# Attention's products as plain 32-bit matmuls, with P times V in column halves

## The chip, the cores and the metric

One core of a Trainium2 chip runs the whole program. The metric is the device time of one execution in microseconds (us), the median of several runs; lower is better. TensorE is called PE in the rows, its weight load PEld, VectorE DVE, ScalarE ACT, GpSimd POOL and SyncE SP.

## The reference

Causal attention over 2 batches, 12 heads, 448 positions and a head size of 64, then two feed-forward layers on its 896 x 768 output:

```python
scores = scale * np.matmul(q, k.transpose(0, 1, 3, 2))
scores = np.where(mask, -1000000000.0, scores)
scores = scores - np.max(scores, axis=-1, keepdims=True)
attn = np.exp(scores)
attn = attn / (np.sum(attn, axis=-1, keepdims=True) + 1e-09)
attn_out = np.matmul(attn, v)
x = attn_out.transpose(0, 2, 1, 3).reshape(896, 768)
x = (1 / (1 + np.exp(-(x @ w_gate))) * (x @ w_val)) @ w_out   # 768 -> 1536 -> 768
h = x @ w_in                                                 # 768 -> 2048
out = (h * np.clip(h + 3, 0, 6) / 6) @ w_out2                # 2048 -> 768
```

q, k and v arrive in 32 bits, the weights in 64 bits.

## The kernel before

Every large product is made of three matmuls. An operand is split into a high part of reduced precision (type fp32r) and the rest, low, also fp32r; `TERMS` (line 22) lists high times high, high times low and low times high, and the product low times low is left out. The attention, the part that changes, works on 12 pairs of heads (`NP`), and both heads of a pair lie side by side on the 128 partitions.

For each pair these steps run, with a short key for each:

- `Lq`, `Lk`, `Lv` (`load`, line 238): SP issues two DMAs for each of q, k, v.
- `Tq`, `Tk` (`t_pe`, line 273): TensorE transposes q and k, 4 pieces each; `Th` and `Tl` (lines 284 and 291) make the high part on ACT and the low part on DVE.
- `Vh`, `Vl` (`v_hi`, `v_lo`, lines 262 and 268): POOL splits v into tiles `vpad` whose other half is zero, so that one matmul serves both heads; these zeros are set once at the start (line 586), half on POOL and half on DVE.
- `S0`, `S1` (`s_pe`, line 299): the scores of four query tiles of 64, 128, 128 and 128 rows against 64, 192, 320 and 448 keys. Each of the three terms is a pair of matmuls on 64 partitions, one for each head (line 309); two or four small bf16 matmuls (line 320) add the causal mask.
- `M`, `E`, `R`, `N` (lines 330 to 356): row maximum on DVE, exponential and row sum on ACT with a small addition at line 343, reciprocal on DVE, division on POOL.
- `C0` to `C3` (`c_pe`, line 358): 16 TensorE transposes of the probabilities, in key chunks of 64 (both heads on the partitions), two chunks in one bank; `H` (line 374) copies the high part out on ACT, `J` (line 380) the low part on DVE.
- `D0` to `D3` (`d_pe`, line 388): P times V, 7 chunks of three matmuls with 448, 384, ... 64 columns, each with all 128 partitions and all 128 output rows.
- `Xh`, `Xl` (lines 406 and 409): the result's parts on ACT and DVE.

The order of all steps is a list written out by hand: a key for each step (`PERIOD`, `SHIFT`, `AT`, `OWN`), and the steps are issued in the order of their keys as far as dependences and buffer rings allow (lines 546 to 568). Three weight tiles of the first layer are decoded in between (`W`, `Wa` to `Wg`), matmuls of that layer that need only the first batch run late in the attention (`F`, 6 steps for each of two tiles, the matmul at line 190), and matmuls on an idle tile (`Z`, line 486) fill the start. After the attention come the two feed-forward layers, line 594 to the end, which the change doesn't touch; weights are decoded there on ACT and DVE while TensorE multiplies (lines 190, 744, 1197).

Of the kernel before, what the change touches and what calls it, by code (L numbers as in the profile page):

```python
# [31 lines left out]
def kernel(  # L32
# [178 lines left out]
    with tc.manual_schedule():  # L211

        with ExitStack() as actx:
            def pool(name, bufs, **kw):
# [11 lines left out]
            identf = const.tile([P, P + D], F32, name="identf")  # L226
# [5 lines left out]
            vpad = [  # L232
                [const.tile([P, NC, P], F32R, name=f"vpad{i}_{x}") for x in range(2)]
                for i in range(NV)
            ]
            live = {}

            def load(p, nm):
                b, hp = divmod(p, NPAIR)
                if nm == "v":  # L240
                    t = p_raw.tile([P, NC, D], F32, tag=nm, name=nm)
                    for j in range(2):
                        nc.sync.dma_start(
                            out=t[j * D : (j + 1) * D],
                            in_=v[b, 2 * hp + j].rearrange("(c p) d -> p c d", p=D),
                        )
                    live[nm, p] = t
# [11 lines left out]
            def halves_of(t):  # L259
                return [t[j * D : (j + 1) * D, :, j * D : (j + 1) * D] for j in range(2)]  # L260

            def v_hi(p):
                for j, hi in enumerate(halves_of(vpad[p % NV][0])):
                    nc.gpsimd.tensor_scalar(
                        hi, live["v", p][j * D : (j + 1) * D], 1.0, 1.0, op0=ALU.mult, op1=ALU.mult
                    )

            def v_lo(p):
                raw = live.pop(("v", p))
                for j, (hi, lo) in enumerate(zip(*(halves_of(t) for t in vpad[p % NV]))):  # L270
                    nc.gpsimd.tensor_sub(lo, raw[j * D : (j + 1) * D], hi.bitcast(F32))
# [12 lines left out]
            def t_hi(p, nm):  # L284
                hi = p_qk.tile([P, S], F32R, tag=nm + "h", name=nm + "h")
                nc.scalar.activation(
                    hi, live["tr", p, nm], AF.Copy, scale=SCALE if nm == "q" else 1.0
                )
                live[nm + "h", p] = hi

            def t_lo(p, nm):
                lo = p_qk.tile([P, S], F32R, tag=nm + "l", name=nm + "l")
                nc.vector.scalar_tensor_tensor(
                    lo, live.pop(("tr", p, nm)), SCALE if nm == "q" else 1.0,
                    live[nm + "h", p].bitcast(F32), op0=ALU.mult, op1=ALU.subtract,
                )
                live[nm + "l", p] = lo

            def s_pe(p, ts):
                both = ps_a.tile([P, 2, 512], F32, tag="m", name="s")  # L300
                off = 0
                for t in ts:
                    rows, n = Q1[t] - Q0[t], Q1[t]
                    ps = both[:, :, off : off + n]
                    off += n
                    for i, (a, c) in enumerate(TERMS):
                        for j in range(2):
                            r = slice(j * D, (j + 1) * D)
                            nc.tensor.matmul(  # L309
                                ps[:, j],  # L310
                                lhsT=live["q" + "hl"[a], p][r, Q0[t] : Q0[t] + P],
                                rhs=live["k" + "hl"[c], p][r, :n],
                                start=(i == 0),
                                stop=(i == 2),
                            )

                    for h in range(rows // D):
                        for j in range(2):
# [4 lines left out]
                                start=False, stop=True, skip_group_check=True,  # L323
                            )
                    live["s", p, t] = ps[:rows]

            def column(tag, t):
                return p_sm.tile([P, 2], F32, tag=tag, name=tag)[: Q1[t] - Q0[t]]

            def s_max(p, t):  # L330
                nm = column("nm", t)
                nc.vector.tensor_reduce(nm, live["s", p, t], axis=AX.X, op=ALU.max, negate=True)  # L332
                live["nm", p, t] = nm

            def s_exp(p, t):
                ps, nm, sm = live.pop(("s", p, t)), live.pop(("nm", p, t)), column("sm", t)
                pr = p_p.tile([P, Q1[t] // D, 2, D], F32, tag=f"pr{t}", name="pr")[: Q1[t] - Q0[t]]
                for j in range(2):
                    nc.scalar.activation(  # L339
                        pr[:, :, j], ps[:, j].rearrange("p (c d) -> p c d", d=D), AF.Exp,  # L340
                        bias=nm[:, j : j + 1], accum_out=sm[:, j : j + 1],
                    )
                nc.scalar.activation(sm, sm, AF.Copy, bias=1e-9)
                live["pr", p, t], live["sm", p, t] = pr, sm

            def s_rcp(p, t):
                sm, rc = live.pop(("sm", p, t)), column("rc", t)
                nc.vector.reciprocal(rc, sm)  # L348
                live["rc", p, t] = rc

            def s_nrm(p, t):
                pr, rc = live["pr", p, t], live.pop(("rc", p, t))
                for j in range(2):
                    nc.gpsimd.tensor_scalar(  # L354
                        pr[:, :, j], pr[:, :, j], rc[:, j : j + 1], 1.0, op0=ALU.mult, op1=ALU.mult
                    )

            def c_pe(p, g):
                ps = ps_pt.tile([P, 512], F32, tag="pt", name="pt")
                for c, off in GROUPS[g]:  # L360
                    for t in range(NQ):
                        if Q1[t] > c * D:


                            r, rows = max(0, c * D - Q0[t]), Q1[t] - Q0[t]
                            o = off + Q0[t] + r - c * D
                            nc.tensor.transpose(  # L367
                                ps[:, o : o + rows],
                                live["pr", p, t][:, c].rearrange("p j d -> p (j d)"),
                                identf[:rows, r : r + rows],  # L370
                            )
                live["pt", p, g] = ps

            def c_hi(p, g):
                m = WIDTH[g]
                hi = p_pt.tile([P, 512], F32R, tag="pth", name="pth")
                nc.scalar.copy(hi[:, :m], live["pt", p, g][:, :m])
                live["pth", p, g] = hi

            def c_lo(p, g):  # L380
                m = WIDTH[g]
                lo = p_pt.tile([P, 512], F32R, tag="ptl", name="ptl")
                nc.vector.tensor_sub(
                    lo[:, :m], live.pop(("pt", p, g))[:, :m], live["pth", p, g][:, :m].bitcast(F32)
                )
                live["ptl", p, g] = lo

            def d_pe(p, g):
                if g == 0:
                    live["pav", p] = ps_1.tile([P, S], F32, tag="pav", name="pav")  # L390
                pt = live.pop(("pth", p, g)), live.pop(("ptl", p, g))
                for c, off in GROUPS[g]:
                    for m, (a, e) in enumerate(TERMS):
                        nc.tensor.matmul(  # L394
                            live["pav", p][:, c * D :],
                            lhsT=vpad[p % NV][a][:, c],
                            rhs=pt[e][:, off : off + S - c * D],
                            start=(c == 0 and m == 0),
                            stop=((c, off) == GROUPS[-1][-1] and m == 2),
                        )  # L400
# [13 lines left out]
            GROUPS, WIDTH, chunks = [], [], list(range(NC))  # L414
            while chunks:
                GROUPS.append([])
                WIDTH.append(0)
                for c in list(chunks):
                    if len(GROUPS[-1]) < 2 and WIDTH[-1] + max(S - c * D, P) <= 512:
                        GROUPS[-1].append((c, WIDTH[-1]))  # L420
                        WIDTH[-1] += S - c * D
                        chunks.remove(c)
# [5 lines left out]
            PERIOD = 33902  # L428
            SHIFT = [
                -9916, -3016, 760, 4313, 10984, 14552, 19678, 24941, 28538, 34564, 37386, 44110,  # L430
            ]
            AT = {
# [831 lines left out]
```

## Time and profile before

| | us |
|---|---|
| median of 3 runs (598.39 to 600.19) | 599.24 |
| the profiled execution | 598.94 |
| its span, first to last instruction | 597.0 |
| PE busy in it | 585.6 |

The profile is of one execution. Its span is 1.9 us shorter than that execution's time, and the profiled execution lies 0.3 us under the median. The busy time of PE comes from modelled ends of overlapping matmuls; the start-to-start time of two matmuls, read from a timeline or from a chain, says what each really takes.

### The profile page before, as it was taken

What the parts mean: (1) busy time and instruction counts of PE and PEld (TensorE: products, weight loads), DVE (VectorE), ACT (ScalarE), POOL (GpSimd) and SP (SyncE); (2) the same over time, 40 slices, a digit from 0 to 9 for tenths busy, and PEclk for the clock granted to TensorE, in tenths of its full rate; (3) what the DMA queues carried; (4) which work ended last, traced back from release to release, by engine and by line L of the source; (5) the groups of instructions that cost most, each with busy time, mean ns of one, the idle gap of its engine ahead of it and who ended that gap; (6) DMA issues with size and microseconds to landing.
All of it is one profiled execution on the core that took longest, in us unless ns stands there. A gap on an engine that the chain in (4) does not pass through costs nothing.

```text
span 597.0 us, 9165 instructions
## 1 busy us (share of the span) xinstructions
PE 585.6 (98%) x3436; PEld 536.0 (90%) x3436; DVE 477.0 (80%) x733; ACT 345.2 (58%) x680; POOL 136.6 (23%) x201
## 2 busy tenths in 40 slices
PE   9999999999999999999999999999999999999997
PEld 5887888999998999898999999988998899999997
DVE  6899988578798898899867788888999988867601
ACT  4998999445665666658343332486777555433200
POOL 2988998601111111110000000012222000000000
PEclk9999999999999999999999999999999999999999
DMA  7664314047986767673344433467978424437002
GB/s 174 158 147 109 86 32 122 2 132 184 264 187 173 208 161 182 171 181 110 99 135 159 143 122 107 111 158 172 245 192 207 133 57 133 128 105 246 7 0 93
DMA packets 86684, 82.64 MB, mean 138 GB/s; under 512 B 35312, under 2 KB 77040, under 8 KB 86640
## 3 DMA queue, kind: packets, MB, share of 16 engines
q1 hardware_dynamic: 80448, 64.50, 36.3%
q0 software_dynamic: 6192, 17.57, 16.0%
q8 instruction: 27, 0.44, 0.3%
q14 instruction: 17, 0.14, 0.1%
HBM read 61.73 MB, written 2.75 MB: 108 GB/s over the span
## 4 chain that ended last, share of the span: by engine, by line
DVE 38%; PE 38%; ACT 18%; issue 5%; DMA 1%; SPq 0%; ACTq 0%; DVEq 0%; POOLq 0%
PE w L744 14%; PE m L1197 12%; DVE b L128 7%; DVE b L134 6%; PE pav L394 4%; DVE lo L158 4%; DVE b L124 4%; ACT hi L153 3%; ACT pr L339 3%; ACT b L115 3%; PE pt L367 2%; DVE g L1165 2%; DVE raw L120 2%; PE s L309 2%; DVE g L182 2%
## 5 line engine op out<-in xcount | busy, mean ns | idle before, releaser
L1197 PE MATMUL m<-hi,g 128*128 128x384 f32 x448 | 114.0, 335 | 0.6 <-DVE g L1165 0.6
L153 ACT CAST hi<-b 128x768 fp32r<-128x768 f32 x35 | 29.0, 835 | 105.6 <-DVE b L134 101.3
L1197 PEld LDWEIGHTS m<-hi,g 128*128 128x128 f32 x448 | 80.8, 188 | 1.2 <-DVE g L1165 1.2
L1197 PE MATMUL m<-lo,g 128*128 128x384 f32 x224 | 75.0, 335 | 0.4 <-DVE lo L158 0.4
L744 PE MATMUL w<-T,hi 128*128 128x448 f32 x252 | 71.9, 367 | 1.4 <-ACT g2r L761 1.4
L190 PE MATMUL m<-g,hi 128*128 128x448 f32 x288 | 70.1, 365 | 0.0
L128 DVE SCALAR_TENSOR_TENSOR b<-b,raw 128x768 int32<-128x768 int32 x68 | 67.0, 985 | 2.2
L134 DVE SCALAR_TENSOR_TENSOR b<-raw,b 128x768 int32<-128x768 int32 x68 | 66.2, 974 | 2.3
L115 ACT ACTIVATE b<-raw 128x768 f32<-128x768 f32 x68 | 61.2, 904 | 0.0
L190 PEld LDWEIGHTS m<-g,hi 128*128 128x128 f32 x288 | 54.1, 188 | 4.3
L124 DVE TENSOR_SCALAR b<-b 128x768 f32<-128x768 f32 x68 | 38.5, 566 | 23.4 <-ACT b L115 23.0
L158 DVE TENSOR_TENSOR lo<-b,hi 128x768 fp32r<-128x768 f32 x35 | 33.4, 958 | 28.1 <-ACT hi L153 28.0
L144 POOL DMA_DIRECT2D lo<-S x26 | 25.2, 971 | 130.9 <-ACT lo L143 110.7
L744 PEld LDWEIGHTS w<-T,hi 128*128 128x128 f32 x252 | 46.9, 188 | 6.0 <-ACT g2r L761 2.1
L354 POOL TENSOR_SCALAR pr<-pr,rc 128x320 f32<-128x320 f32 (+3 forms) x96 | 45.4, 489 | 16.7 <-DVE rc L348 14.3
L190 PE MATMUL m<-x,hi 128*128 128x448 f32 x192 | 48.9, 367 | 0.0
L744 PE MATMUL w<-T,lo 128*128 128x448 f32 x126 | 46.3, 367 | 0.9 <-DMA lo<-raw 0.6
L339 ACT ACTIVATE pr<-s,nm 128x192 f32<-128x192 f32 (+3 forms) x96 | 44.4, 470 | 2.6 <-DVE nm L332 1.6
L1197 PEld LDWEIGHTS m<-lo,g 128*128 128x128 f32 x224 | 42.0, 188 | 0.7 <-DVE lo L158 0.7
L394 PE MATMUL pav<-pth,vpad 128*128 128x448 f32 (+6 forms) x168 | 41.2, 311 | 0.1
L190 PE MATMUL m<-g,lo 128*128 128x448 f32 x144 | 40.9, 366 | 0.0
L190 PEld LDWEIGHTS m<-x,hi 128*128 128x128 f32 x192 | 35.9, 188 | 2.8
(140 smaller groups left out, 1249.4 us busy)
## 6 DMA issues: line engine op xcount, KB each, us to landing
raw<-in_moe_w_out_dram SPq DMA_DIRECT2D x28, 768.0 KB, 4.4
raw<-in_moe_w_in_dram SPq DMA_DIRECT2D x16, 768.0 KB, 4.7
lo<-S POOLq DMA_DIRECT2D x26, 384.0 KB, 4.3
raw<-in_moe_w_gate_dram SPq DMA_DIRECT2D x12, 768.0 KB, 5.0
raw<-in_moe_w_val_dram SPq DMA_DIRECT2D x12, 768.0 KB, 5.1
q<-in_q_dram SPq DMA_DIRECT2D x24, 112.0 KB, 2.9
k<-in_k_dram SPq DMA_DIRECT2D x24, 112.0 KB, 3.2
v<-in_v_dram SPq DMA_DIRECT2D x24, 112.0 KB, 2.8
```

What stands on the lines that cost most here:

```text
L115: nc.scalar.activation(b, words(u)[0].bitcast(F32), AF.Copy, scale=REBIAS)
L124: nc.vector.tensor_scalar(b, b, UPPER_MAX, -UPPER_MAX, op0=ALU.min, op1=ALU.max)
L128: nc.vector.scalar_tensor_tensor(bi, bi, 3, words(u)[1], op0=ALU.logical_shift_left, op1=ALU.bitwise_or)
L134: nc.vector.scalar_tensor_tensor(bi, words(u)[0], -(2 ** 31), bi, op0=ALU.bitwise_and, op1=ALU.bitwise_or)
L153: nc.scalar.copy(hi, part_t[u])
L158: nc.vector.tensor_sub(lo, part_t.pop(u), split_t[u][0].bitcast(F32))
L190: nc.tensor.matmul(ps[:, b, :S], lhsT=w[a][:, i * P : (i + 1) * P], rhs=x(c, k0 + i, b), start=(first and i == 0 and n == 0), stop=(last a ...
L339: nc.scalar.activation(pr[:, :, j], ps[:, j].rearrange("p (c d) -> p c d", d=D), AF.Exp, bias=nm[:, j : j + 1], accum_out=sm[:, j : j + 1],)
L354: nc.gpsimd.tensor_scalar(pr[:, :, j], pr[:, :, j], rc[:, j : j + 1], 1.0, op0=ALU.mult, op1=ALU.mult)
L394: nc.tensor.matmul(live["pav", p][:, c * D :], lhsT=vpad[p % NV][a][:, c], rhs=pt[e][:, off : off + S - c * D], start=(c == 0 and m == 0), ...
L744: nc.tensor.matmul(ps, lhsT=w[a][:, k * P : (k + 1) * P], rhs=x[:, c, i], start=(first and i == 0 and n == 0), stop=(i == HK - 1 and n == ...
L1197: nc.tensor.matmul(po[t], lhsT=g2[2 * s + i][a][:, t * P : (t + 1) * P], rhs=w[e][:, i * HC : (i + 1) * HC], start=(s == 0 and i == 0 and ...
```

## The change

Scores and P times V are each one matmul on plain 32-bit operands in place of three on split ones. For the scores there are then 2 matmuls for each query tile, one a head, after the mask's matmuls instead of before them. For P times V the key chunks become one of 64 keys and three of 128 keys. The chunk of 64 still serves both heads with one matmul; a chunk of 128 takes two matmuls, one a head, that use all 128 partitions and write 64 output partitions each: the two column halves of the array. These are 7 matmuls with 448, 384, 384, 256, 256, 128 and 128 columns. The transposes of the probabilities stay 16.

The splits of v, the low parts of q, k and P, and the high copies go; q comes out by ACT, k by DVE, two of the four groups of transposed probabilities by ACT and two by DVE. V goes by four DMAs a pair straight into three rotating 32-bit tiles, whose zeros are 6 blocks of 64 x 64 instead of 12 of 64 x 448. The addition and the reciprocal of the row sums handle two query tiles at once. The idle tile's matmuls read a constant, and the list of keys is another one.

```diff
--- before.py
+++ after.py
-            vpad = [
-                [const.tile([P, NC, P], F32R, name=f"vpad{i}_{x}") for x in range(2)]
-                for i in range(NV)
-            ]
+            vs = [const.tile([P, NQ, 2, D], F32, name=f"v{i}") for i in range(NV)]
...
             def load(p, nm):
                 if nm == "v":
-                    t = p_raw.tile([P, NC, D], F32, tag=nm, name=nm)
                     for j in range(2):
-                        nc.sync.dma_start(
-                            out=t[j * D : (j + 1) * D],
-                            in_=v[b, 2 * hp + j].rearrange("(c p) d -> p c d", p=D),
-                        )
+                        chunks = v[b, 2 * hp + j].rearrange("(c p) d -> p c d", p=D)
+                        for x in range(2):
+                            nc.sync.dma_start(
+                                out=vs[p % NV][x * D : (x + 1) * D, x != j :, j],
+                                in_=chunks[:, x != j :: 2],
+                            )
...
-            def v_hi(p):
-            def v_lo(p):
-            def t_hi(p, nm):
-            def t_lo(p, nm):
+            def t_out(p, nm):
+                t = live[nm + "t", p] = p_qk.tile([P, S], F32, tag=nm + "t", name=nm + "t")
+                if nm == "q":
+                    nc.scalar.activation(t, live.pop(("tr", p, nm)), AF.Copy, scale=SCALE)
+                else:
+                    nc.vector.tensor_copy(t, live.pop(("tr", p, nm)))
...
             def s_pe(p, ts):
-                    for i, (a, c) in enumerate(TERMS):
-                        for j in range(2):
-                            r = slice(j * D, (j + 1) * D)
-                            nc.tensor.matmul(
-                                ps[:, j],
-                                lhsT=live["q" + "hl"[a], p][r, Q0[t] : Q0[t] + P],
-                                rhs=live["k" + "hl"[c], p][r, :n],
-                                start=(i == 0),
-                                stop=(i == 2),
-                            )
...
+                for t in ts:
+                    for j in range(2):
+                        r = slice(j * D, (j + 1) * D)
+                        nc.tensor.matmul(
+                            live["s", p, t][:, j],
+                            lhsT=live["qt", p][r, Q0[t] : Q0[t] + P],
+                            rhs=live["kt", p][r, : Q1[t]],
+                            start=False, stop=True, skip_group_check=True,
+                        )
...
+            def s_eps(p, g):
+                sm = live["sm", p, g]
                 nc.scalar.activation(sm, sm, AF.Copy, bias=1e-9)
...
-            def c_hi(p, g):
-            def c_lo(p, g):
-            def d_pe(p, g):
+            def c_out(p, g):
+                m, ps = WIDTH[g], live.pop(("pt", p, g))
+                t = live["pth", p, g] = p_pt.tile([P, 512], F32, tag="pth", name="pth")
+                if g % 2:
+                    nc.vector.tensor_copy(t[:, :m], ps[:, :m])
+                else:
+                    nc.scalar.copy(t[:, :m], ps[:, :m])
+
+            def d_pe(p, d):
+                if d == 0:
                     live["pav", p] = ps_1.tile([P, S], F32, tag="pav", name="pav")
+                pav, pt = live["pav", p], {g: live.pop(("pth", p, g)) for g in DSTEPS[d]}
+                for i, j, off, g in sorted((*b, g) for g in DSTEPS[d] for b in GROUPS[g]):
+                    w, r, x = S - Q0[i], slice(j * D, (j + 1) * D), vs[p % NV][:, i]
+                    nc.tensor.matmul(
+                        pav[r, Q0[i] :] if i else pav,
+                        lhsT=x[:, j] if i else x.rearrange("p j d -> p (j d)"),
+                        rhs=pt[g][:, off : off + w],
+                        start=(i == 0), stop=True, skip_group_check=True,
+                    )
...
+            GROUPS = [
+                [(0, 0, 0)], *([(1, j, 0), (3, j, S - Q0[1])] for j in range(2)),
+                [(2, j, j * (S - Q0[2])) for j in range(2)],
+            ]
+            DSTEPS = [(0,), (1, 2), (3,)]
...
-            PERIOD = 33902
+            PERIOD = 21033
```

## Rows read from the trace of the kernel before

**Rows 1.** The page: busy time, share of the span and instructions by engine.
```profile
PE 585.6 (98%) x3436; PEld 536.0 (90%) x3436; DVE 477.0 (80%) x733; ACT 345.2 (58%) x680; POOL 136.6 (23%) x201
```

**Rows 2.** Stretches: length, busy PE, PEld, DVE, ACT, POOL, granted clock, DMA share, GB/s.
```profile
0.00:58.45 58.45, 55.67 (x496) 42.99 (x496) 49.26 (x102) 47.06 (x159) 43.26 (x77) 1.00 0.62 148
58.45:119.68 61.23, 61.23 (x548) 54.55 (x549) 48.97 (x101) 49.83 (x171) 51.26 (x82) 1.00 0.24 61
...
83.67:92.13 8.46, 8.46 (x85) 7.41 (x84) 6.99 (x17) 7.78 (x28) 7.96 (x15) 1.00 0.21 48
119.68:250.00 130.32, 129.70 (x640) 119.82 (x640) 112.95 (x159) 79.58 (x110) 20.35 (x21) 1.00 0.73 186
```

**Rows 3.** The chain that ended last, 100 to 300 us: start, us, what.
```profile
106.13 1.30 PE m L190 x6
...
112.27 3.65 PE m L190 x18
...
116.79 2.87 PE pav L394 x21
...
251.09 22.24 PE w L744 x108
```

**Rows 4.** The same chain over one pair of heads, 74.67 to 83.13 us, by line.
```profile
by line: PE pav L394 35.5%; PE s L309 25.8%; PE pt L367 23.5%; PE tr L277 11.1%; PE s L320 4.1%
```

**Rows 5.** PE's timeline, 59.6 to 66 us: start, us, instruction.
```profile
59.77 0.28 PE L309 MATMUL s<-kh,ql 64*128 64x64 f32 x2
59.89 0.21 PE L320 MATMUL s<-maskb,identb 64*128 64x64 bf16 x2
...
60.21 0.37 PE L309 MATMUL s<-kl,qh 64*128 64x448 f32 x2
60.42 0.37 PE L309 MATMUL s<-kh,ql 64*128 64x448 f32 x2
...
61.10 0.34 PE L394 MATMUL pav<-ptl,vpad 128*128 128x384 f32 x1
61.28 0.41 PE L394 MATMUL pav<-pth,vpad 128*128 128x384 f32 x2
...
64.17 0.28 PE L394 MATMUL pav<-ptl,vpad 128*128 128x256 f32 x1
64.28 0.32 PE L394 MATMUL pav<-pth,vpad 128*128 128x256 f32 x2
...
64.95 0.27 PE L309 MATMUL s<-kl,qh 64*128 64x192 f32 x2
65.06 0.28 PE L309 MATMUL s<-kh,ql 64*128 64x192 f32 x2
...
65.50 0.31 PE L309 MATMUL s<-kl,qh 64*128 64x320 f32 x2
65.65 0.31 PE L309 MATMUL s<-kh,ql 64*128 64x320 f32 x2
```

**Rows 6.** The timeline of the start, 0 to 30 us.
```profile
3.01 3.25 DVE L586 MEMSET vpad<- 64x448 f32 x6
...
6.83 0.61 DVE L293 SCALAR_TENSOR_TENSOR kl<-tr,kh 128x448 fp32r<-128x448 f32 x1
7.03 1.37 SPq L243 DMA_DIRECT2D v<-in_v_dram  x2
...
9.33 0.45 PE L309 MATMUL s<-kh,qh 64*128 64x192 f32 x2
```

**Rows 7.** Groups by line and shape, 0 to 119.68 us: busy us, mean ns, idle before.
```profile
L377 ACT CAST pth<-pt 128x512 fp32r<-128x512 f32 x24 | 14.0, 582 | 3.8 <-PE pt L367 3.6
L343 ACT ACTIVATE sm<-sm 128x2 f32<-128x2 f32 x36 | 7.3, 204 | 1.1
...
L383 DVE TENSOR_TENSOR ptl<-pt,pth 128x512 fp32r<-128x512 f32 x24 | 16.3, 679 | 4.0 <-ACT pth L377 4.0
...
L271 POOL TENSOR_TENSOR vpad<-v,vpad 64x448 fp32r<-64x448 f32 x24 | 29.9, 1246 | 1.9
```

More of the change, by code (lines that the diff above doesn't have):

```diff
@@ L322, in s_pe, with column @@
                                 rhs=maskb[r, j * D : (j - h) * D + rows],
-                                start=False, stop=True, skip_group_check=True,
+                                start=(t == ts[0] and h == 0), stop=True, skip_group_check=True,
                             )
-                    live["s", p, t] = ps[:rows]
-            def column(tag, t):
-                return p_sm.tile([P, 2], F32, tag=tag, name=tag)[: Q1[t] - Q0[t]]
+                for t in ts:
+                    for j in range(2):
[6 more added lines that the diff above has]
+                        )
+            def column(tag):
+                return p_sm.tile([P, 2, 2], F32, tag=tag, name=tag)
             def s_max(p, t):
-                nm = column("nm", t)
+                nm = column("nm")[:, 0]
                 nc.vector.tensor_reduce(nm, live["s", p, t], axis=AX.X, op=ALU.max, negate=True)
@@ L359, in c_pe @@
                 ps = ps_pt.tile([P, 512], F32, tag="pt", name="pt")
[L360 to L371, printed above, removed]
@@ L388, in d_pe @@
-            def d_pe(p, g):
-                if g == 0:
-                    live["pav", p] = ps_1.tile([P, S], F32, tag="pav", name="pav")
[L391 to L400, printed above, removed]
+                for i, j, off in GROUPS[g]:
+                    for t in range(i, NQ):
+                        n, rows, o = Q1[t], Q1[t] - Q0[t], off + Q0[t] - Q0[i]
+                        c = n + Q0[i] if j else n - Q1[i]
+                        nc.tensor.transpose(
+                            ps[:, o : o + P], live["pr", p, t].rearrange("p j n -> p (j n)")[:, c : c + P],
+                            identf,
+                        )
@@ L473 @@
                     add(f"E{t}", [f"M{t}"], s_exp, t)
-                    add(f"R{t}", [f"E{t}"], s_rcp, t)
-                    add(f"N{t}", [f"R{t}"], s_nrm, t)
+                for i, ts in enumerate(STILES):
+                    add(f"Q{i}", [f"E{t}" for t in ts], s_eps, i)
+                    add(f"R{i}", [f"Q{i}"], s_rcp, i)
+                    for t in ts:
+                        add(f"N{t}", [f"R{i}"], s_nrm, t)
                 for g in range(NG):
-                    tiles = [f"N{t}" for t in range(NQ) if Q1[t] > GROUPS[g][0][0] * D]
+                    tiles = [f"N{t}" for t in range(GROUPS[g][0][0], NQ)]
                     add(f"C{g}", tiles, c_pe, g)
-                    add(f"H{g}", [f"C{g}"], c_hi, g)
-                    add(f"J{g}", [f"H{g}"], c_lo, g)
-                    add(f"D{g}", [f"J{g}", "Vl", f"D{g - 1}"][: 2 + (g > 0)], d_pe, g)
-                add("Xh", [f"D{NG - 1}"], x_hi)
+                    add(f"H{g}", [f"C{g}"], c_out, g)
+                for d, gs in enumerate(DSTEPS):
+                    add(f"D{d}", [*(f"H{g}" for g in gs), "Lv", *[f"D{d - 1}"][: d]], d_pe, d)
+                add("Xh", [f"D{len(DSTEPS) - 1}"], x_hi)
                 add("Xl", ["Xh"], x_lo)
             def z_pe(p):
-                nc.tensor.matmul(idle_ps, lhsT=idle[:, :P], rhs=idle, start=True, stop=True)
+                nc.tensor.matmul(idle_ps, lhsT=ones[:, :P], rhs=ones, start=True, stop=True)
             for i in range(len(WARM)):
@@ L524, in every @@
                 return [((p, a), [(p, x) for x in z]) for p in range(NP) for a, *z in uses]
-            last = [
-                max(g for g in range(NG) if GROUPS[g][0][0] * D < Q1[t]) for t in range(NQ)
-            ]
+            last = [max(g for g in range(NG) if GROUPS[g][0][0] <= t) for t in range(NQ)]
+            dstep = {g: d for d, gs in enumerate(DSTEPS) for g in gs}
             rings = [
@@ L540 @@
                 *((2, every((f"E{t}", f"C{last[t]}"))) for t in range(NQ)),
-                (2, every(*((f"C{g}", f"J{g}") for g in range(NG)))),
-                (4, every(*((f"H{g}", f"D{g}") for g in range(NG)))),
+                (2, every(*((f"C{g}", f"H{g}") for g in range(NG)))),
+                (4, every(*((f"H{g}", f"D{dstep[g]}") for g in range(NG)))),
                 (2, [((NP - 3, f"Wa{u}"), [(NP - 3, f"Wg{u}")]) for u in range(3)]),
@@ L579 @@
             )
-            nc.vector.tensor_copy(identb, identf)
+            for c, w in ((0, P), (P, D)):
+                nc.vector.tensor_copy(identb[:, c : c + w], identf[:, :w])
             nc.vector.tensor_copy(maskb, maskf)
-            for i, pair in enumerate(vpad):
-                for x, t in enumerate(pair):
-                    eng = nc.gpsimd if 2 * i + x < 3 else nc.vector
-                    for j in range(2):
-                        eng.memset(
-                            t[j * D : (j + 1) * D, :, (1 - j) * D : (2 - j) * D].bitcast(F32), 0.0
-                        )
+            for t in vs:
+                for j in range(2):
+                    nc.vector.memset(t[(1 - j) * D : (2 - j) * D, 0, j], 0.0)
             emit_in_order()
```

103 lines of the change are left out of this document (33 added, 70 removed), and 23 rows, old and new, of tables (AT, OWN).

## Prediction

> **What bounds the kernel now.** I read the stretches first. PE is busy nearly all the time [rows 1], but its ends are modelled, so I look at start-to-start times. After the attention TensorE runs 448-column matmuls at 3.65 / 18 = 0.203 us [rows 3] and still at 22.24 / 108 = 0.206 us far behind it [rows 3], at a granted clock of 1.00, the level of 2.4 GHz [rows 2]. So the feed-forward layers are limited by TensorE, nothing there is changed, and what the attention gains or loses moves the end by as much. From 58.45 us until P times V ends (116.79 + 2.87 = 119.66 us [rows 3]) TensorE never idles [rows 2], and the chain over one pair of heads, 8.46 us, lies on TensorE alone [rows 4]. By line these are 3.00 us of P times V, 2.18 of scores, 1.99 of transposed probabilities, 0.94 of transposed q and k, and 0.35 of mask. ACT and POOL are not far off, with 7.78 and 7.96 us busy in such a period [rows 2].
>
> Twelve pairs at 8.46 are 101.5 us, and the 24 early matmuls of the first layer [rows 3] are 4.9. So of 119.66 us TensorE loses 13.3, all before 58.45: in the start, where the first scores come at 9.33 us [rows 6], and while the other engines, ACT at 47.06 of 58.45 us busy [rows 2], set the pace.
>
> **TensorE's part of the change.** Transposes and mask keep their instructions: 1.99 + 0.94 + 0.35 = 3.28 us a pair. The trace of before has no plain 32-bit product. Its own split says what one must contain: each operand has a high and a low half, so the full product is four half-products, of which the kernel now issues three. I take a plain matmul as four passes of the same shape at the pitch of the fp32r rows. For one pass of both heads' scores the pitch is 0.12 us at 64 keys, 0.11 at 192, 0.15 at 320 and 0.21 at 448 [rows 5], both heads starting together (each row counts two). That sums to 0.59, four passes to 2.36 us, against 2.18 now. For P times V a pass takes 0.20 at 448 columns [rows 3], 0.18 at 384 and 0.11 at 256 [rows 5]. For 128 columns I take 0.11 too, since 64 columns also take 0.12 [rows 5]. If the two column halves run side by side as the two heads' row halves do, that is 0.60 a pass and 2.40 us in all, against 3.00. The gain is there because 7 chunks become 4, and narrow ones cost a floor that wide ones don't. TensorE's pair becomes 3.28 + 2.36 + 2.40 = 8.04 us, 0.42 less, and twelve pairs are 96.5.
>
> The bounds: if the passes of one matmul follow each other without any floor, 1024 score columns and 1216 of P times V at four passes and 2.4 GHz are 1.71 + 2.03 = 3.74, a pair 7.02. From above, if no two heads overlap, twice the scores and the paired part are 4.72 + 4.00, a pair 12.0; without the floor, 2048 and 1984 columns, 3.41 + 3.31, a pair 10.0. I take 8.04 because the passes of the rows already carry their weight loads.
>
> The Trainium skill, FP8 and Floating Point Precision, section TensorE Precision Notes, says that true FP32 takes four passes through the array, high and low halves in all combinations. No row of this trace shows it; by it the sum would be the one above.
>
> **The other engines.** ACT loses two of four high copies (0.58 each at most), one copy of q or k, and two of four small additions at 0.20 [rows 7]: some 1.9 us of 7.78, so about 5.9 a pair. DVE loses two of four low parts (0.68 [rows 7]), the low part of q and two reciprocals, some 2 us of 6.99. POOL loses both splits of v, of which the subtraction alone is 2 x 1.25 us [rows 7], so at least 2.5 of 7.96. All then lie well under TensorE's 8.04, which also covers them if a copy is no faster than the subtraction it replaces. SP issues four DMAs for v instead of two at 1.37 / 2 = 0.69 us [rows 6]: 1.4 us more a pair on a queue that needs about 5 of 8. It delays the second pair's q by 1.4 us if it stands ahead, while TensorE still waits for the first softmax.
>
> **The start.** Now the zeros hold DVE from 3.01 to 6.26, and the low part of k ends at 7.44 [rows 6]. Without these the first scores can start some 2.6 us sooner, about 6.7. Behind them one chain of maximum, exponential, division, transpose and copy must still pass before P times V. With ACT less loaded I take 8.5 us lost instead of 13.3; the ends are 6.7 (nothing lost once scores start) and 13.3.
>
> **The sum.** 8.5 + 4.9 + 96.5 = 109.9 instead of 119.66, 9.8 less. On the profiled execution 598.94 - 9.8 = 589.1, and with the 0.3 by which the median lies above it, 589.4 us.
>
> **Rivals.** *No floor.* With 7.02 a pair the gain is 12 x 1.02 more: 577. For it: a wide 4-pass matmul may hide its weight loads better than three short ones; against: the fp32r floors at 64 to 256 columns are there [rows 5].
>
> *Half an overlap.* The two heads' passes are issued one after another. If a matmul runs as two bursts of two passes, the second head starts beside the first one's second burst, and each group of query tiles or chunks has one burst standing alone: at the pitches above 0.30 + 0.42 for the scores and 0.36 + 0.22 for P times V, 1.30 us a pair, 15.6 in all: 605. Without the floors the same pattern gives 8.2 a pair, so 591. For it: now the second head follows after one pass, and the overlap is seen for single passes only [rows 5].
>
> *Column halves one after the other*, the case that makes it slower: each head's P times V matmul uses all partitions, and only the output halves differ. If they don't run side by side, 4 x (0.18 + 0.11 + 0.11) = 1.60 us a pair come on top, 19.2 in all: 608.6. It decides from a pair of (119.66 - 8.5 - 4.9) / 12 = 8.85 us on, that is once scores and P times V take over 5.57 together. For it: no row shows column halves, only row halves [rows 5]. If the row halves fail too, it is 613 (no floor) to 637.
>
> The Trainium skill, TensorE: Matmul & The Clock Gate, Part 3, says that a weight load overlaps running matmuls only when its row group differs; by it the second head's weights, on the same rows, would wait, which is this rival. The same part reports 2.38 times the speed for three column tiles, which speaks against it. No row here shows either.
>
> *The gain is given back.* The attention ends earlier, but the decoding of weights behind it isn't ready, since DVE is busy 112.95 of 130.32 us there [rows 2]. Then little changes: 599. Against it: the three first tiles are decoded during the attention, on engines that become freer.
>
> **How the numbers follow.** Forecast 0.45 (583 to 596 by the start's ends), no floor 0.12, half an overlap 0.18, column halves in turn 0.10, neither overlap 0.08, given back 0.05, anything else 0.02. The range 577 to 609 leaves out the slow case without overlap and the edges of the first and third rival. A measurement of this kernel tells about 0.3% (1.8 us) from no change: faster 0.59, same 0.08, slower 0.33. Both signs hold much; the forecast's own range is 583 to 596.
>
> **What would show it.** In the chain over one late pair: period about 8.0, scores 2.4, P times V 2.4. In TensorE's timeline: both heads' 384-column matmuls starting together (right) or one whole matmul apart (column rival) or half of one (half overlap). In the stretches: ACT near 5.9 a period and POOL near 4 to 5. In the start: first scores near 6.7 us. And behind the attention the pitch still at 0.203 to 0.206; if it is longer there, the gain is given back. The prediction is wrong if a plain matmul isn't four passes, or if the halves don't overlap.

## The result and the profile after

The median is 591.27 us (591.23 to 592.41, 4 runs) against 599.25 us (598.39 to 600.19, 4 runs): a ratio of 0.987, 95% interval 0.985 to 0.989. The profiled execution took 591.24 us instead of 598.94, 7.7 less, with a span of 589.5.

The page of after, busy time by engine, answers to [rows 1]:

```profile
PE 576.6 (98%) x3254; PEld 505.6 (86%) x3255; DVE 450.8 (76%) x672; ACT 326.7 (55%) x620; POOL 90.4 (15%) x147
```

The stretches of after, with the columns of [rows 2]; the attention ends at 109.25 us:

```profile
0.00:22.00 22.00, 19.96 (x142) 11.67 (x143) 9.22 (x26) 11.95 (x42) 6.77 (x20) 1.00 0.61 145
22.00:84.00 62.00, 60.41 (x539) 38.74 (x538) 47.75 (x91) 52.33 (x182) 33.21 (x65) 1.00 0.51 116
84.00:109.25 25.25, 24.75 (x182) 16.58 (x181) 13.24 (x25) 13.89 (x47) 9.12 (x20) 1.00 0.27 79
109.25:250.00 140.75, 138.33 (x679) 126.89 (x679) 121.42 (x170) 84.93 (x118) 21.09 (x22) 1.00 0.73 184
```

TensorE now has idle time in the second and third row, where before it had none from 58.45 us on [rows 2]. In the chain that ended last (start us, us, what; from the view of 0 to 125 us) the start and the end of eight pairs can be read, and between them, from 39.3 us on, the chain lies mostly on ACT and DVE:

```profile
26.68 0.28 PE s L285 x8
...
27.90 0.53 PE tr L260 x4
...
57.51 1.25 ACT pr L317 x4
...
59.70 0.62 DVE x L382
60.32 1.19 DVE nm L305 x2
...
90.08 0.28 PE s L285 x8
...
109.25 15.80 PE m L190 x77
```

The same view of 84.5 to 110 us, where the chain is TensorE's again, answers to [rows 3] and [rows 4]:

```profile
85.17 0.22 PE s L285 x6
85.39 1.06 PE s L293 x8
86.45 1.04 PE pt L347 x8
87.49 0.76 PE pav L367 x2
88.25 0.39 PE tr L260 x4
88.63 1.45 PE pav L367 x12
90.08 0.28 PE s L285 x8
90.36 0.95 PE s L293 x8
...
93.44 0.87 PE pt L347 x8
...
107.06 2.20 PE pav L367 x14
```

From these rows a pair's parts are: scores 1.06 + 0.95 = 2.01 us (2.18 before [rows 4]), mask 0.22 + 0.28 = 0.50 (0.35 before), P times V 0.76 + 1.45 = 2.21 (3.00 before), transposed probabilities 1.04 + 0.87 = 1.91. Adding the transposes of q and k, 0.53 + 0.39 = 0.92 in the same chain, makes 7.55 us. But the eight pairs from 26.68 to 90.08 us took 63.40 / 8 = 7.92 each: in the middle TensorE isn't what sets the pace.

So P times V ends at 107.06 + 2.20 = 109.25 us instead of 119.66 [rows 3], 10.4 earlier. Twelve pairs are 12 x 0.91 = 10.9 less; the 24 early matmuls take 5.05 instead of 4.9 (three pieces of the same chain, 3.24 + 1.21 + 0.60); and TensorE loses 109.25 - 5.05 - 12 x 7.55 = 13.6 us, against 13.3 before. From there to the end it takes 2.9 us longer than before (589.5 - 109.25 = 480.2, before 597.0 - 119.66 = 477.3), and most of this is one wait in TensorE's timeline behind the attention (start us, us, instruction, idle time before it in brackets):

```profile
155.49 0.98 PE L190 MATMUL m<-x,hi 128*128 128x448 f32 x4
158.35 0.67 PE L190 MATMUL m<-x,lo 128*128 128x448 f32 x2 [1.88 <-DMA lo<-b]
```

Right behind the attention the pitch is as before (15.80 / 77 = 0.205 us); some 0.8 of the 2.9 us lie in small differences of both signs far behind, which no run here explains. The tile waited for is a later one: the DMA of its low part is issued on POOL at 152.47 us, 43.2 us after the attention's end, and before it was issued at 161.18, 41.5 us after it. The program decodes these tiles in turn behind the third one, and the third one is late, for its decoding on DVE stands behind the last pair's `Xl`. DVE's timeline of after:

```profile
109.87 0.63 DVE L382 TENSOR_TENSOR x<-pav,x 128x448 fp32r<-128x448 f32 x1 [2.68 <-ACT x L379]
110.41 0.55 DVE L124 TENSOR_SCALAR b<-b 128x768 f32<-128x768 f32 x1
111.00 0.96 DVE L128 SCALAR_TENSOR_TENSOR b<-b,raw 128x768 int32<-128x768 int32 x1
111.99 0.96 DVE L134 SCALAR_TENSOR_TENSOR b<-raw,b 128x768 int32<-128x768 int32 x1
```

Before, the first two of these three decoding steps had run ahead of the last `Xl`, and only the third came after it:

```profile
120.79 0.95 DVE L134 SCALAR_TENSOR_TENSOR b<-raw,b 128x768 int32<-128x768 int32 x1
```

### The profile page after: what moved, and what is told of

The parts are those of the page before. It is cut to its first block, busy times and chain, and to the rows that moved or that the text cites. A ratio compares the mean times of both kernels' runs of the same rounds, so it can differ in the third digit from the quotient of the medians.

```text
span 589.5 us, 8611 instructions
## 1 busy us (share of the span) xinstructions
PE 576.6 (98%) x3254; PEld 505.6 (86%) x3255; DVE 450.8 (76%) x672; ACT 326.7 (55%) x620; POOL 90.4 (15%) x147
## 4 chain that ended last, share of the span: by engine, by line
PE 60%; DVE 22%; ACT 12%; issue 3%; DMA 2%; ACTq 0%; DVEq 0%
PE m L190 26%; PE w L705 13%; PE m L1158 12%; DVE b L128 3%; ACT pr L317 3%; PE pav L367 2%; DVE g L1126 2%; ACT b L115 2%; DVE b L134 2%; PE s L293 2%; DVE b L124 2%; PE pt L347 2%; DVE nm L305 2%; DVE lo L158 2%; DMA g<-b 1%
## 5 line engine op out<-in xcount | busy, mean ns | idle before, releaser
L128 DVE SCALAR_TENSOR_TENSOR b<-b,raw 128x768 int32<-128x768 int32 x68 | 65.3, 960 | 2.4
L337 POOL TENSOR_SCALAR pr<-pr,rc 128x192 f32<-128x192 f32 (+3 forms) x96 | 47.9, 516 | 53.6 <-DVE rc L329 42.6
L120 DVE TENSOR_SCALAR raw<-raw 128x768 int32<-128x768 int32 x68 | 37.7, 554 | 0.0
```

What stands on the lines that cost most here:

```text
L120: nc.vector.tensor_scalar(lower, lower, 29, None, op0=ALU.logical_shift_right)
L128: nc.vector.scalar_tensor_tensor(bi, bi, 3, words(u)[1], op0=ALU.logical_shift_left, op1=ALU.bitwise_or)
L337: nc.gpsimd.tensor_scalar(pr[:, j], pr[:, j], rc[:, j : j + 1], 1.0, op0=ALU.mult, op1=ALU.mult)
```

## The experiments

Every kernel is given as its median, its range and its ratio to runs of before on the same chip. The question after the result was twofold: is the gain what the prediction says it is (the plain products, the column halves), and what took back a part of it (the middle, the wait behind)?

### What took back a part

**The third weight tile's decoding, moved forward as one block.** An edit of after:

```diff
-... "Wc2": 422716,
-... "Wd2": 422717, ... "We2": 422718,
-... "Wf2": 425621, ... "Wg2": 684075,
+... "Wc2": 306001,
+... "Wd2": 306002, ... "We2": 306003,
+... "Wf2": 306004, ... "Wg2": 306005,
```

> The changed kernel with one thing else: the decoding of the third weight tile (its steps Wc2 to Wg2) stands in the list ahead of the last pairs' steps, where VectorE has idle time, and no longer behind the last pair's output. Theory: in the changed kernel TensorE waits 1.9 us at 158 us for a weight tile because this decoding starts 1.5 us late behind the attention; without it that wait goes and the time is 589.4, 1.9 less than 591.3. Rival: that wait is the transfer's own, 5.8 us from issue to landing; then nothing changes, 591.3.

590.96 us (590.16 to 591.47), ratio 0.987 (0.984 to 0.989). The wait near 156 us is gone, and what follows the attention is 2.1 us shorter (474.1 to the last matmul instead of 476.2). But P times V ends at 111.57 us, 2.3 later, so the expected 589.4 wasn't reached. The place of the decoding is the wait's cause; moved as a block it costs the attention what it saves behind it. Up to 90 us the attention is as in after (the last pair's mask matmuls start at 89.99 us in TensorE's timeline, in after at 90.01). The loss lies in the last pair: in the chain of 84 to 113 us the decoding stands between that pair's second and third maximum.

```profile
94.66 0.48 DVE b L124
...
98.03 0.96 DVE lo L158
```

**The mask issued twice: more work for TensorE alone.**

```diff
+                for again in range(2):
                   for t in ts:
```

> The changed kernel with the mask's small matmuls issued twice, which adds 0.50 us of TensorE work a pair and nothing else. Theory: between 22 and 84 us TensorE is no longer what sets the pace, so only the start and the last three pairs pay: 592.5 to 594. Rival (TensorE sets it everywhere, as the prediction's sum has it): 12 x 0.50 = 6.0 us more, 597.3.

591.47 us (591.16 to 591.90), ratio 0.988 (0.985 to 0.991). The chain of this kernel, 84 to 95 us:

```profile
86.41 0.34 PE s L286 x12
...
91.41 0.45 PE s L286 x16
```

A second issue costs 0.34 - 0.22 = 0.12 and 0.45 - 0.28 = 0.17, so 0.29 us a pair, less than the 0.50 that the expectations were made with, and 3.5 us in twelve pairs. Of these 1.35 show in the end of P times V (110.60). TensorE has room for over half of it: it isn't the bound in the middle, which supports the reading above. The time itself grew by only 0.2 us, and missed the expected 592.5 to 594, because the wait near 158 us is 0.77 us here instead of 1.88.

**Without the row maximum.** The maximum is left out, and the exponential's bias is a constant zero:

```diff
-                nm = column("nm")[:, 0]
-                nc.vector.tensor_reduce(nm, live["s", p, t], axis=AX.X, op=ALU.max, negate=True)
+                nm = zero
```

> The changed kernel without the row maximum: the exponential takes a bias of zero, VectorE loses four reductions a pair (2.7 us), and the exponential no longer waits for VectorE. Theory: in the middle of the attention the chain through VectorE and ScalarE (reciprocal of one pair, then the next pair's maximum, then its exponential) sets the pace; without it TensorE's own 7.55 us a pair does, and the time falls by 4 to 7 us, to 584 to 587. Rival (TensorE sets the pace already): 591, within 1 us.

586.05 us (585.06 to 587.86), ratio 0.979 (0.976 to 0.982). P times V ends at 103.78 us, 5.5 earlier. The stretch of this kernel:

```profile
22.00:84.00 62.00, 62.00 (x558) 40.72 (x558) 31.31 (x60) 53.59 (x188) 34.19 (x67) 1.00 0.51 117
```

TensorE never idles here, and ACT is as busy as in after (53.59 against 52.33 us), DVE much less (31.31 against 47.75). What held the middle thus goes with the maximum, by DVE's time or by the wait for it, and isn't ACT's load alone. Eight pairs now take (84.88 - 24.66) / 8 = 7.53 us each, by the first mask matmuls in TensorE's timeline, and the lost time is 103.78 - 5.05 - 12 x 7.53 = 8.4 us. That this is near the prediction's 8.5 is chance, since the prediction kept the maximum.

**The maximum computed, but not used.** To part the wait for the maximum from DVE's load, the exponential reads a constant zero, and the reduction stays:

```diff
-                ps, nm = live.pop(("s", p, t)), live.pop(("nm", p, t))
+                ps, nm = live.pop(("s", p, t)), zero
```

> The changed kernel with the row maxima still computed, but the exponential takes a bias of zero and no longer waits for them. Without the maxima altogether the attention was 5.5 us shorter. Theory: it is the wait (maximum behind the last pair's reciprocal, exponential behind the maximum) that costs, not VectorE's 2.7 us a pair: 586 to 588. Rival (VectorE's load): 590 to 592.

591.52 us (591.06 to 592.84), ratio 0.986 (0.984 to 0.989), no different from after. But it doesn't part them: in the list of waits (engine and line, waited for: us in total, times, longest us) of 22 to 84 us the exponential still waits for the reduction (both read the same scores; what asks for the wait isn't shown):

```profile
ACT pr L317 <- DVE nm L305: 4.8, 9, 1.1
```

The same row stands in the list of after. Whether the wait or the load counts stays open by this run.

**The reciprocal a third of a period later.** In the waits of after, the longest totals hang on the joined reciprocal (line 329), which waits for ACT's row sums and holds DVE's queue:

```profile
POOL pr L337 <- DVE rc L329: 19.2, 12, 3.8
DVE rc L329 <- ACT sm L325: 10.1, 9, 2.2
```

So its second group was put further back:

```diff
-... "R1": 24549, ...
+... "R1": 36549, ...
```

> The changed kernel with one key of the list moved: the reciprocal of the second group of query tiles comes behind the next pair's first maximum instead of ahead of it, where VectorE waits for ScalarE's sums while ScalarE then waits for the maximum. Theory: this order costs ScalarE about 1 us in most pairs, so the time falls by 2 to 5 us: 586 to 589. Rival (TensorE sets the pace, or the wait moves to the transposes that need the division): within 1 us of 591.3, or slower.

592.86 us (592.65 to 593.70), ratio 0.991 (0.988 to 0.993), P times V ends at 111.0, 1.8 later than in after. The theory that this wait blocks the maximum behind it wanted it faster by 2 to 5 us. The wait of line 329 did go from the head of the list, but others took its place: POOL waits longer for the reciprocal (26.8 us instead of 19.2), and the weight loads of TensorE's transposes wait longer for POOL's divisions (5.8 instead of 2.1).

```profile
POOL pr L337 <- DVE rc L329: 26.8, 14, 3.5
PEld pt L347 <- POOL pr L337: 5.8, 10, 1.3
```

So this move doesn't help, and a large total in the list of waits isn't by itself a gain to be had. Whether the reciprocal's wait costs time where it stood isn't shown, since the move delays the division as well.

**The third tile's steps spread between the last pairs.** The same steps as in the first experiment, one or two at a time:

```diff
-... "Wc2": 422716,
-... "Wd2": 422717, ... "We2": 422718,
-... "Wf2": 425621, ... "Wg2": 684075,
+... "Wc2": 324780,
+... "Wd2": 324781, ... "We2": 344272,
+... "Wf2": 365323, ... "Wg2": 365325,
```

> The changed kernel with the third weight tile's decoding put into the gaps that the trace shows at the attention's end: two VectorE steps after the last reciprocal but one copy, the others each behind a copy of the last pair. Earlier placement ended the wait at 156 us but made the attention 2.3 us longer. Theory: in these gaps the steps cost the attention nothing, P times V ends at 109.1 to 109.6 as in the changed kernel, the 2.2 us wait behind it is gone, and the time is 589.3 (1.5 to 2.5 less than 591.3). Rival: the engines' order is so tight that the attention grows by as much again, within 0.7 of 591.3.

589.02 us (588.40 to 589.25), ratio 0.982 (0.980 to 0.984). P times V ends at 109.38 us, as in after, and the wait is gone: in the same timeline the matmuls follow each other without idle time.

```profile
155.62 0.98 PE L190 MATMUL m<-x,hi 128*128 128x448 f32 x4
156.43 0.57 PE L190 MATMUL m<-x,lo 128*128 128x448 f32 x2
```

2.2 us of the attention's gain had been given back there; that is shown.

### Where the gain comes from

**The column halves in another order.** The matmuls of one step are issued head by head (384, 128, then 384, 128 columns) instead of in couples:

```diff
-                for i, j, off, g in sorted((*b, g) for g in DSTEPS[d] for b in GROUPS[g]):
+                for i, j, off, g in sorted(
+                    ((*b, g) for g in DSTEPS[d] for b in GROUPS[g]), key=lambda b: (b[1], b[0])
+                ):
```

> The changed kernel with the P times V matmuls of the chunks of 384 and 128 columns issued head by head, so that two neighbours use the same column half and can't run side by side except at one place. Theory: P times V then takes 1.60 us instead of 0.95 for these eight passes, 0.65 more a pair on TensorE; since TensorE doesn't set the pace in the middle, 2 to 4 us more: 593 to 595. Rival (TensorE sets it everywhere): 7.8 more, 599. Second rival (column halves don't really overlap, the near starts in the trace are only queueing): no change, 591.3.

591.78 us (590.98 to 593.43), ratio 0.989 (0.986 to 0.992). It was meant to take the overlap away, and didn't: the twelve records still take 1.45 us in the chain. TensorE's timeline:

```profile
88.39 0.87 PE L369 MATMUL pav<-pth,v 128*64 128x384 f32 x4
```

Four records of 384 columns, both heads', start with none of 128 columns between them, though the program has the first head's 128 columns ahead of the second head's 384; the two heads' first records start 13 ns apart. So the order in the program doesn't part the halves. The time is that of the second rival (no change), but the next run shows that the rival's reason, no overlap, isn't why.

**P times V at full width.** Each matmul reads both heads' columns of V and writes all 128 output rows, so that no two can run side by side; the two heads' outputs are mixed by it, while count and columns stay:

```diff
-                        pav[r, Q0[i] :] if i else pav,
-                        lhsT=x[:, j] if i else x.rearrange("p j d -> p (j d)"),
+                        pav[:, Q0[i] :],
+                        lhsT=x.rearrange("p j d -> p (j d)"),
```

> The changed kernel with each P times V matmul on all 128 output rows in place of a column half (each head's probabilities multiply both heads' values, so the two heads' outputs are mixed and the result is another one); count and columns are the same, but no two run side by side. Theory: at 2.4 GHz and four passes the six narrower ones take 2.56 us a pair in place of 1.45 for the three overlapped couples, about 1.2 us more on TensorE; 0.50 more made the attention 1.35 us longer, so TensorE has some slack and then none: 5 to 9 us more, 596 to 600. Rival (TensorE's time hardly matters): under 594. Second rival (TensorE sets the pace everywhere): 14 more, 605.

602.36 us (600.24 to 603.19, 10 runs), ratio 1.0035 (1.0019 to 1.0050). From the chain of this kernel, 55 to 70 us:

```profile
59.76 2.60 PE pav L367 x12
```

The same six matmuls take 2.60 us instead of 1.45, and P times V ends at 119.3 us, some 10 later than in after, where 5 to 9 were expected. TensorE now sets the pace in the middle: by the first mask matmuls in its timeline eight pairs take (97.04 - 27.54) / 8 = 8.69 us each, and 7.55 + 1.15 is 8.70. The overlap of the halves is worth as much as the whole gain: without it the change would be slower by 0.35%.

**The plain scores alone.** Before, with its split P times V, and the scores as plain matmuls:

```diff
-                    for i, (a, c) in enumerate(TERMS):
-                        for j in range(2):
...
+                    for j in range(2):
+                        r = slice(j * D, (j + 1) * D)
+                        nc.tensor.matmul(
+                            ps[:, j],
+                            lhsT=live["qt", p][r, Q0[t] : Q0[t] + P],
+                            rhs=live["kt", p][r, :n],
+                            start=True, stop=True, skip_group_check=True,
+                        )
```

> The kernel before with the scores alone as plain 32-bit matmuls (q copied out by ScalarE, k by VectorE); P times V, V's splits and the list of keys as before. Theory: TensorE's pair loses the 0.17 us that the rows after show for the scores (2.18 to 2.01), 2.0 us in all, and the start some 1 us by the missing low parts: 596 to 597. Rival (a plain matmul is dearer on TensorE beside split products, or the four passes cost more than three): 599 or more.

600.84 us (599.52 to 603.83, 10 runs), ratio 1.0040 (1.0021 to 1.0059). One pair in the chain, the second half:

```profile
73.84 0.37 PE s L300 x4
74.21 0.03 PE s L310 x2
74.24 0.83 PE s L300 x4
75.07 0.08 PE s L310 x4
```

With the first half's 0.53 and 0.62 the scores are 2.35 us a pair, the mask 0.30: 2.65 in all, against 2.53 before [rows 4] and 0.50 + 2.01 = 2.51 in after. For TensorE the plain scores are no gain, and the expected 596 to 597 wasn't reached. P times V still ends 2.5 us earlier (117.17), with the splitting of q and k off the other engines; from there to the last matmul it takes 4.1 us more than before, spread over the layers, and the cause stays open.

**P times V alone.** After, with split scores as before it:

```diff
-            def t_out(p, nm):
+            def t_hi(p, nm):
...
+            def t_lo(p, nm):
...
+                    for i, (a, c) in enumerate(TERMS):
+                        for j in range(2):
```

> The changed kernel with the scores back to three split matmuls (the low parts of q and k again on VectorE, k's high part on ScalarE); P times V, V by DMA and the list as changed. Theory: the scores' part is worth little (TensorE 0.17 us a pair), but VectorE and ScalarE, which now set the pace in the middle, get 0.6 and 0.5 us a pair more: 593 to 596. Rival (TensorE alone counts): 12 x 0.17 = 2.0 more, 593.3, with ScalarE and VectorE no matter.

614.00 us (612.68 to 615.20), ratio 1.025 (1.021 to 1.029): a miss, and not a clean price. Its stretch of 22 to 84 us:

```profile
22.00:84.00 62.00, 53.90 (x485) 37.62 (x485) 40.36 (x77) 43.12 (x148) 24.85 (x50) 0.94 0.42 95
```

TensorE idles 8.1 of 62 us, and the mean granted clock is 0.94. The new list brings k out shortly before its scores (keys -17750 and -4248, before -49891 and -21343), so the split's extra step lands in the chain that must pass before them (in the list of waits of 20 to 100 us DVE's low part of k waits 14.0 us for its high part on ACT); no cost of P times V can be read from it.

**After's computation in before's list.** The new steps stand where the old ones stood:

```diff
-            PERIOD = 21033
+            PERIOD = 33902
...
-                "C0": 51676, "C1": 51677, "C2": 72728, "C3": 72729, "D0": 80715, "D1": 91157, "D2": 91158, "E0": 14972,
+                "C0": 51462, "C1": 51463, "C2": 71116, "C3": 71117, "D0": 71825, "D1": 79622, "D2": 92035,
```

> The changed kernel's computation in the order of the list of the kernel before (its period, shifts, keys and fillers; the new joint steps stand behind the later of the two they replace). Theory: the new list is a good part of the gain, since what the attention takes is set by waits between VectorE and ScalarE in program order: 595 to 603. Rival (the products and the saved copies bring it, the list little): 590 to 593.

588.74 us (585.99 to 589.68), ratio 0.981 (0.978 to 0.984): a clear miss of the expectation that the new list brings a good part. P times V ends at 108.03 us, 1.2 sooner than in after. The stretch of this kernel and one pair of its chain:

```profile
22.00:84.00 62.00, 62.00 (x550) 39.14 (x549) 51.03 (x92) 52.44 (x182) 31.18 (x64) 1.00 0.50 119
```

```profile
66.25 0.28 PE s L285 x8
...
68.88 0.75 PE pav L367 x2
...
70.91 1.01 PE pav L367 x8
...
73.33 0.58 PE pav L367 x4
73.92 0.16 PE s L285
```

TensorE never idles, and the whole pair lies on it, 73.92 - 66.25 = 7.67 us, with DVE and ACT as busy as in after (51.03 and 52.44 us). So it is not their load alone that slows after's middle but the order in which they are asked; the lost time is 108.03 - 5.05 - 12 x 7.67 = 10.9 us, not 13.6. The products bring the gain, and the new list costs some 2.5 us of it: 1.2 in the attention, the rest behind it, where this list has no wait near 156 us.

**The same, with the last three couples of P times V joined.** In the period above P times V takes 0.75 + 1.01 + 0.58 = 2.34 us; in one piece it takes 2.21.

```diff
-... "D1": 79622, "D2": 92035,
+... "D1": 92034, "D2": 92035,
```

> The changed kernel's computation in the list of the kernel before, as in the earlier run, with one key moved: the second step of P times V comes directly ahead of the third, so that the six column-half matmuls of a pair stand together. Theory: with this list TensorE sets the pace from 14 us on, at 7.67 us a pair, so TensorE time saved moves the end: standing apart the two steps take 1.01 + 0.58 = 1.59 us, together 1.45, so 0.14 a pair and 1.7 in all: P times V ends near 106.2 in place of 107.9, and the time is 587.1 in place of 588.7. Rival: VectorE and ScalarE take the pace back when the step comes later, and the end stays at 107.9 or comes later.

587.65 us (587.37 to 588.11, 5 runs), ratio 0.981 (0.979 to 0.983). Its interval lies below that of after (0.985 to 0.989), so this version beats both kernels; against the run before it the last step is within the error. Two starts of a pair and one joined P times V, from its chain of 56 to 81 us, and a new wait from 84 to 110:

```profile
57.58 0.28 PE s L285 x8
...
63.83 1.45 PE pav L367 x12
...
80.31 0.28 PE s L285 x8
```

```profile
86.56 1.85 POOL pr L337 x4
...
90.18 2.55 POOL pr L337 x4
```

(80.31 - 57.58) / 3 = 7.58 us a pair: TensorE's sum of 7.55 is reached. P times V ends at 107.22 us, 0.8 sooner instead of the expected 1.7, as two divisions on POOL now end last near 90 us.

## Why the prediction was right, and where its terms were off

The forecast was 589.4 us, 9.8 less on the profiled execution; it was 7.7 less. The mechanism holds, two terms of the sum were off in opposite directions, and a rival of small chance came in part.

- **The layers behind pass the attention's saving on.** Right but for one wait: their pitch right behind the attention is unchanged, and 10.4 us saved in the attention became 7.7. The prediction gave 0.05 to the case that the decoding isn't ready. In part it came: 2.2 us, at one tile behind the third, and moving the third tile's steps gave it back (589.02). The step that failed is that all three first tiles are decoded inside the attention. The new list leaves two more steps of the third one behind its end.
- **Four half-products.** Right. Each plain matmul is two MATMUL records in the trace (48 of 448 columns in 12 pairs, for two heads), each of about twice the columns in time: the 448 columns of P times V take 0.75 to 0.76 us, which is 4 x 448 / 2400. The Trainium skill, FP8 and Floating Point Precision, section TensorE Precision Notes, says four passes; the time agrees with it.
- **The floor of narrow passes.** Mis-sized. The prediction put every pass at its fp32r row: scores 2.36 us, P times V 2.40. Without any floor they are 4 x 1024 / 2400 = 1.71 and 4 x 1216 / 2400 = 2.03. Measured were 2.01 and 2.21, about half way. The mask, taken at 0.35, costs 0.50 where it now stands, ahead of the scores in one piece; with plain scores and the mask in its old place it took 0.30. The pair is 7.55 us instead of 8.04, 5.9 us less in twelve.
- **Halves side by side.** Right, and the step on which the gain rests: three couples in 1.45 us, with 4 x 768 / 2400 = 1.28 as their least, and 2.60 at full width. In the records of after both heads' passes start 5 to 7 ns apart for the column halves, and 3 or 4 ns apart for most of the row halves. This refutes both *half an overlap* and *column halves one after the other*. The Trainium skill, TensorE: Matmul & The Clock Gate, Part 3, has a weight load overlap only when its row group differs; here the row group is the same (each half uses all 128 partitions), yet the first couple's four weight loads start at 88.56 us and end at 88.76, while its second passes start only at 88.94, and the couples run 2.60 / 1.45 = 1.79 times as fast. The measurement decides.
- **P times V brings the gain, the scores nothing.** Right: 0.79 us a pair against 0.02 for scores and mask together, and the plain scores alone didn't make the kernel faster. The reason given, fewer chunks that pay a floor, is most of it. Before, the seven chunks had 1792 columns and three matmuls each, by the same estimate at least 3 x 1792 / 2400 = 2.24 us, and 3.00 were taken, 0.76 more; now the least is 2.03, and 2.21 are taken, 0.18 more. So about 0.58 of the 0.79 is overhead and 0.21 fewer column passes. No run has split operands on the column halves, so what the plain operands do by themselves, apart from the new chunks and halves, isn't shown.
- **Lost time 8.5 us.** Wrong: 13.6, just beyond the upper end of 13.3. The first scores came at 7.46 us, not 6.7, but that isn't the reason: in the run with the third tile's steps spread they came at 6.74, with the same start in the program, and P times V ended at 109.38, no sooner than in after. In the middle 8 x (7.92 - 7.55) = 3.0 us go where the prediction had none. The step that failed is that the other engines "lie well under TensorE's 8.04". It counted ACT at 5.9 us and DVE at about 5 for the pair alone. In the stretch of 22 to 84 us ACT is busy 52.33 / 62 x 7.92 = 6.7 us a period and DVE 6.1, since weights are decoded there too, and TensorE's period is 7.55, not 8.04. Yet load alone didn't decide: with the same load in the old list TensorE never idles there (10.9 us lost), and without the maximum 8.4 are lost. Busy shares below one hid a chain, maximum to exponential to sum to reciprocal, that passes between DVE and ACT several times a pair; which of its steps counts isn't shown. The other 2.1 us of the 5.1 lie ahead of 26.68 us or behind 90.08, and no run parts them.

So the sum landed near by luck: a smaller pair (-5.9) and a larger loss (+5.1) nearly cancelled, and 2.2 us given back made most of the rest.

## What to carry to other kernels

Where two products with few output rows share an input's partitions, plain 32-bit matmuls on the two column halves of the array can beat three split ones, because they run side by side and fewer, wider chunks pay less overhead; a version at full width shows what that is worth. Once TensorE's part shrinks, look again at who is next: at a busy share of 0.84 a chain between two engines can set the pace, and a new order of steps has to be timed against the old order with the same computation, as its cost can hide in the gain. Of a saving in one stage ask which step at its border was hidden by the old, longer stage.

## What the runs showed of the hardware

- A plain 32-bit matmul appears as two weight loads and two MATMUL records, and at 448 columns takes 4 columns' time for each column at 2.4 GHz (granted clock 1.00): 0.75 us. At 64 columns it took more than that: both heads' scores 0.25 us (85.23 to 85.48 in TensorE's timeline), against 4 x 64 / 2400 = 0.11.
- In the run with the column halves in another order, matmuls on the two halves didn't keep the program's order between the halves: the second head's 384 columns started 13 ns after the first head's, ahead of the first head's 128 columns, which stand earlier in the program.
- A second issue of the mask's small bf16 matmuls right behind the first cost 0.12 and 0.17 us where the first cost 0.22 and 0.28.
